# Hashed attention and two gated layers on one core: q and k arrive as columns, twice over, and the hash bits come from one fp32 product a head

## The chip, the cores and the metric

One core of one Trainium2 chip runs the whole program. The metric is device time in microseconds (us). The kernel before takes 852.57 us, the median of 3 runs (852.17 to 852.62). TensorE is PE in the rows (its weight loads are PEld), VectorE is DVE, ScalarE is ACT, GpSimd is POOL, and SyncE, which issues all transfers, is SP. SBUF is the on-chip memory, PSUM the accumulators that TensorE writes.

## The reference

q, k and v are 2 batches x 8 heads x 768 rows x 64. Six hash bits put each row of q and of k in one of 64 buckets; a score counts only where the buckets agree. Two layers with a gate follow.

```
q_bucket = sum over i of 2^i * ((q @ proj)[..., i] > 0)      # k_bucket likewise
scores   = where(q_bucket == k_bucket, q @ k.T / 8, -1e9)
attn     = exp(scores - max);  attn /= sum(attn) + 1e-9
x        = (attn @ v), heads side by side: 1536 x 512
xn       = x / sqrt(mean(x*x) + 1e-6) * rms_g
y        = (silu(xn @ w_gate) * (xn @ w_val)) @ w_out        # 512 -> 1536 -> 512
h        = y @ w2_in;  out = where(h > 0, h, exp(h) - 1) @ w2_out   # 512 -> 2048 -> 512
```

## The kernel before

**Numbers.** Products run in fp32r, a shorter float that TensorE takes at a quarter of fp32's passes. To keep precision each operand is split into a "hi" (the cast) and a "lo" (the value less its cast), and the products of the parts are summed.

**Stages.** Heads are taken in 8 pairs. For each pair there is a *preparation*, which makes the score operands `tq` and `tk` of both heads, then 12 score blocks (128 rows of q against 768 of k; matmul `ps_s` L477, maximum `nm` L484 on VectorE, exponential L494 on ScalarE), the transposes of the probabilities (`ps_p` L522), their split into `pt` (L530 and L534, or L539, L543 and L546 by way of GpSimd), and the product with v (`ps_v` L569). When 4 pairs are done, a batch is normalized (`norm`, and `post` for each pair). The two layers follow (`ps_h` L908, `ps_y` L993, `ps_o` L1048) in 5 + 6 groups of weights; the weights come as float64 words, are put together as fp32 in `wf` by VectorE (L814 to L834), cast to `whi` (L855) and split to `wlo` on GpSimd (L859).

**A pair's preparation.** q and k come with rows on the partitions (`raw`, L276). `twice` (L334, GpSimd) copies each 64-wide row beside itself. `prep_T` transposes 128x128 blocks on TensorE (`ps_t`, L350), so that 128 partitions hold the 64 columns twice. From PSUM ScalarE makes hi (L356), VectorE makes lo (L361, one operand in PSUM and one in SBUF), and GpSimd copies halves about (`again` L368, `across` L371). `prep_bits` (L398, L403) multiplies the operands with `pj`, three products of parts a head and half; `prep_count` (L419, L428, L430) turns the bits into the 64 mask rows that stand in the operands' other half. A score block needs all of these of its head. Pair j + 1 is prepared while pair j is scored.

**What sets the order.** Each piece of work is a task with an engine, a time, what it reads and writes, and a priority. `Plan.order` (L77) walks through the tasks and gives each engine the one that can start first, the lowest priority number first among equals; it holds back tasks for which no buffer is free. The order comes out as a fixed list for each engine, and each engine takes its list strictly in turn. `OFF` (L33) holds the offsets to the priorities, by stage and pair. The buffers are `slot` (24 of 6 KB a partition: operands, probabilities, weights, layer inputs), `h3` (9 of 3 KB: `rd`, `vn`, `pf`, `wf` and others), and in PSUM 4 banks and 2 double banks.

Of the kernel before, what the change touches and what calls it, by code (L numbers as in the profile page):

```python
# [32 lines left out]
OFF = {'S': [-0.746, -0.843, -1.864, 66.85, -0.744, -0.758, -0.224, -0.41], 'max': [86.06, 128.957, 190.513, 53.124, 102.143, -5.035, -10.834, 24.749], 'exp': [119.567, 67.059, 76.291, 2.774, 75.069, 56.662, -35.846, 43.868], 'T': [0.573, 0.48, 0.307, 0.831, 0.703, 1.127, 1.259, 1.321], 'hi': [36.303, -33.663, 1.961, -57.136, 22.322, 57.959, -91.469, -121.974], 'lo': [-34.121, 9.653, 32.465, -109.77, -12.636, -87.223, -67.192, -11.818], 'V': [2.027, 1.953, 1.894, 2.015, 1.865, 2.222, 2.417, -11.303], 'my': [76.979, -114.216, -55.16, -8.134, -134.423, -45.978, -63.486, -29.752], 'ld': [16.116, 103.645, 134.666, -130.684, 51.199, 277.906, -45.786, 44.455], 'pv': [19.903, -68.605, 49.828, -156.296, 63.827, 116.499, -168.838, 19.653], 'prep': [-0.809, -2.78, -3.346, -0.341, -0.21, -0.194, 0.226, -82.459], 'post': [4.851, 4.774, 2.643, 1.592, 3.332, 9.244, 3.712, 28.29], 'plo': [-227.264, -10.728, 0.013, -54.307, -64.379, -36.39, 74.399, -48.961], 'wc': 0.693, 'ld1': 50.459, 'norm0': -125.474, 'rush': 27.318, 'pstep': 0.316, 'qstep': 0.146, 'norm': -8.853, 'w0': 189.461, 'w0s': 3.7229545865993564e+29}  # L33
# [146 lines left out]
def kernel(  # L180
    ctx: ExitStack,
    tc: tile.TileContext,
    q: bass.AP,
    k: bass.AP,
    v: bass.AP,
    proj: bass.AP,
    w_gate: bass.AP,
# [82 lines left out]
    def load_qk(j, prio, gate=()):  # L270
        b, h0 = divmod(2 * j, H)

        def go(i, a):
            if ("raw", j) not in st:
                st["raw", j] = slot([128, 2, 2, NC, D], F32, "raw")
            nc.sync.dma_start(  # L276
                out=st["raw", j][:, i, a], in_=(q, k)[i][b, h0 + a].rearrange("(p c) d -> p c d", c=NC)
            )

        for a in range(2):  # L280
            for i in range(2):
                dma(
                    lambda i=i, a=a: go(i, a), S * D * 4, r=[("go", j - 2), *gate],
                    w=[(("slot", "raw", j), i, a)], prio=prio + 0.05 * a,
                )

    def load_v(j, prio):
        b, h0 = divmod(2 * j, H)

# [5 lines left out]

        dma(go, 2 * S * D * 4, r=[("go", j - 1)], w=[("h3", "vn", j)], prio=prio)
# [31 lines left out]
    def twice(j, a, i, prio):  # L328
        eng = FIRST[2 * a + i] if j == 0 else "Pool"

        def go():
            st["rd", j, a, i] = half([128, NC, 2, D], F32, "rd")
            cp = {"Pool": nc.gpsimd.tensor_copy, "DVE": nc.vector.tensor_copy, "ACT": nc.scalar.copy}[eng]
            cp(out=st["rd", j, a, i], in_=st["raw", j][:, i, a].unsqueeze(2).to_broadcast([128, NC, 2, D]))  # L334

        us = {"Pool": POOL_COPY, "DVE": dve(S), "ACT": act(S) + 0.04}[eng]
        plan.add(eng, us, go, [(("slot", "raw", j), i, a)], [("h3", "rd", j, a, i)], prio)

    def prep_T(j, a, i, hf, prio):
        n = NC // 2  # L340
        cs = slice(hf * HS, (hf + 1) * HS)
        sc = QSCALE if i == 0 else 1.0
        B_ = ("bank", "t", j, a, i, hf)
        up, dn = slice(0, 64), slice(64, 128)

        def pe():
            st[B_] = bank("ps_t")
            x = st["rd", j, a, i]
            for c in range(n):
                nc.tensor.transpose(  # L350
                    out=st[B_][:, c * 128:(c + 1) * 128], identity=ident,
                    in_=x[:, hf * n + c].rearrange("p a d -> p (a d)"),
                )

        def hi():
            nc.scalar.activation(out=operand(j, a, i)[:, 0, cs], in_=st[B_][:, 0:HS], func=AF.Copy, scale=sc)  # L356

        def lo():
            t = operand(j, a, i)
            m = (up, slice(0, 128))[i]  # L360
# [12 lines left out]
        plan.add("PE", n * 0.109, pe, [("h3", "rd", j, a, i), "ident"], [B_], prio, duty=0.5)
        top = [okey(j, a, i, (h, hf)) for h in ("up", "dn")]
        plan.add("ACT", act(HS), hi, [B_], top, prio)
        if i == 0:
            plan.add("DVE", dve(HS), lo, [B_], top[:1], prio)
            plan.add("Pool", POOL_HALF, again, top[1:], [okey(j, a, i, ("dup", hf))], prio)
        else:
            plan.add("DVE", dve(HS), lo, [B_, *top], [okey(j, a, i, ("lo", hf)), okey(j, a, i, ("hot", hf))], prio)  # L380
            plan.add("Pool", POOL_HALF, across, [okey(j, a, 0, ("dn", hf))], [okey(j, a, 1, ("hot", hf))], prio)
# [82 lines left out]
    def score(u, cc, prio):  # L464
# [35 lines left out]
        need = skeys(j, a, 0, c // 3) + [okey(j, a, 0, (p, c // 3)) for p in ("dup", "hot")]  # L500
        need += [k for hf in range(2) for k in [*skeys(j, a, 1, hf), okey(j, a, 1, ("hot", hf))]]
# [532 lines left out]
    def reduce_cols(g, blk, t, tt, ds, prio):  # L1034
# [45 lines left out]
    def setup():  # L1080
        make_identity(nc, ident)
        nc.gpsimd.memset(f(pj), 0.0)

    def ones_of(t, i):
        return t.rearrange("p (n t w) -> p n t w", t=2, w=2 ** i)[:, :, 1, :]

    def setup_w():
        st["wtmp"] = half([1, NB, NBK], F32, "wtmp")
        nc.vector.memset(st["wtmp"], -1.0)
        for i in range(NB):  # L1090
            nc.vector.memset(ones_of(st["wtmp"][:, i, :], i), 1.0)

    def setup_count():
        st["ctmp"] = half([1, 2, 2, NBK], F32, "ctmp")
        c = st["ctmp"]
        nc.vector.tensor_reduce(
# [170 lines left out]
```

## Time and profile before

| | |
|---|---|
| median of the runs | 852.57 us |
| span of the profiled execution | 851.1 us |
| busy in the span: TensorE, VectorE | 832.4 us (98%), 638.5 us (75%) |
| busy in the span: ScalarE, GpSimd | 444.9 us (52%), 273.3 us (32%) |
| read from memory, written | 45.09 MB, 3.15 MB |

The profile is of one execution; its span runs from the first to the last instruction. Busy time of a matmul is modelled to its end, and matmuls overlap one another, so a busy TensorE is not one at its peak. Shares over the whole span mix stages: the attention, up to about 300 us, keeps four engines occupied, and the layers behind it mainly TensorE.

### The profile page before, as it was taken

What the parts mean: (1) busy time and instruction counts of PE and PEld (TensorE: products, weight loads), DVE (VectorE), ACT (ScalarE), POOL (GpSimd) and SP (SyncE); (2) the same over time, 40 slices, a digit from 0 to 9 for tenths busy, and PEclk for the clock granted to TensorE, in tenths of its full rate; (3) what the DMA queues carried; (4) which work ended last, traced back from release to release, by engine and by line L of the source; (5) the groups of instructions that cost most, each with busy time, mean ns of one, the idle gap of its engine ahead of it and who ended that gap; (6) DMA issues with size and microseconds to landing.
All of it is one profiled execution on the core that took longest, in us unless ns stands there. A gap on an engine that the chain in (4) does not pass through costs nothing.

```text
span 851.1 us, 12464 instructions
## 1 busy us (share of the span) xinstructions
PE 832.4 (98%) x4722; PEld 736.7 (87%) x4722; DVE 638.5 (75%) x1015; ACT 444.9 (52%) x838; POOL 273.3 (32%) x289
## 2 busy tenths in 40 slices
PE   8999999998999999999999999999999999999998
PEld 7999999887998899999889898887888888888786
DVE  6999899999999987534364565579857778676754
ACT  6988988898987664432222322235444333332321
POOL 7857476789824312111011111110201101111100
PEclk9999999999999999999999999999999999999999
DMA  5102012330002200310111312213121302001003
GB/s 168 41 17 75 2 38 75 121 122 1 20 1 75 75 13 26 112 50 1 56 48 46 100 50 100 75 33 128 62 75 37 112 25 75 25 30 46 1 12 137
DMA packets 25708, 49.05 MB, mean 58 GB/s; under 512 B 2480, under 2 KB 8880, under 8 KB 25648
## 3 DMA queue, kind: packets, MB, share of 16 engines
q1 hardware_dynamic: 25648, 48.25, 17.3%
q8 instruction: 37, 0.61, 0.3%
q14 instruction: 23, 0.19, 0.1%
HBM read 45.09 MB, written 3.15 MB: 57 GB/s over the span
## 4 chain that ended last, share of the span: by engine, by line
PE 81%; DVE 13%; ACT 4%; issue 1%; POOL 1%; ACTq 0%; DVEq 0%; POOLq 0%
PE ps_h L908 37%; PE ps_o L1048 14%; PE ps_y L993 11%; PE ps_p L522 5%; PE ps_v L569 5%; PE ps_s L477 4%; DVE nm L484 3%; DVE pt L534 3%; PE ps_t L350 2%; PE ps_b L398 2%; ACT p L494 1%; ACT pt L530 1%; DVE wf L827 1%; DVE wf L834 1%; PE ps_w L1153 1%
## 5 line engine op out<-in xcount | busy, mean ns | idle before, releaser
L859 POOL TENSOR_TENSOR wlo<-wf,whi 128x768 fp32r<-128x768 f32 (+1 forms) x54 | 86.8, 1607 | 442.9 <-ACT whi L855 430.6
L908 PE MATMUL ps_h<-xn,whi 128*128 128x512 f32 (+2 forms) x768 | 190.2, 337 | 0.8 <-DVE hf L939 0.7
L908 PEld LDWEIGHTS ps_h<-xn,whi 128*128 128x128 f32 x768 | 133.5, 189 | 13.2 <-DVE hf L939 1.1
L908 PE MATMUL ps_h<-xn,wlo 128*128 128x256 f32 (+2 forms) x384 | 128.9, 336 | 0.0
L1048 PE MATMUL ps_o<-whi,h 128*128 128x512 f32 (+1 forms) x388 | 118.7, 387 | 0.8 <-DVE oa L1060 0.8
L908 PE MATMUL ps_h<-y,whi 128*128 128x512 f32 x384 | 118.2, 389 | 0.0
L933 ACT ACTIVATE sg<-ps_h 128x512 f32<-128x512 f32 (+1 forms) x87 | 50.7, 583 | 116.6 <-PE ps_h L908 114.5
L855 ACT CAST whi<-wf 128x768 fp32r<-128x768 f32 (+1 forms) x54 | 39.6, 733 | 118.2 <-DVE wf L834 118.2
L569 PE MATMUL ps_v<-pt,vv 128*128 128x256 f32 x576 | 96.8, 295 | 4.1 <-DVE pt L534 3.2
L954 ACT CAST h<-hf 128x512 fp32r<-128x512 f32 (+1 forms) x87 | 51.6, 605 | 88.1 <-DVE hf L939 49.1
L993 PE MATMUL ps_y<-h,whi 128*128 128x512 f32 (+1 forms) x312 | 91.4, 374 | 1.5 <-DVE ya L1005 1.5
L484 DVE TENSOR_REDUCE nm<-ps_s 128x1 f32<-128x768 f32 x96 | 90.6, 945 | 1.6 <-PE ps_s L477 0.9
L958 DVE TENSOR_TENSOR h<-hf,h 128x512 fp32r<-128x512 f32 (+1 forms) x87 | 71.0, 831 | 26.9 <-ACT h L954 26.2
L494 ACT ACTIVATE p<-ps_s,nm 128x768 f32<-128x768 f32 x96 | 87.2, 909 | 5.5 <-DVE nm L484 4.4
L522 PE MATMUL ps_p<-ident,p 128*128 128x128 f32 x576 | 86.0, 275 | 3.3 <-DVE pt L534 1.5
L477 PE MATMUL ps_s<-tk,tq 128*128 128x384 f32 x384 | 87.9, 350 | 0.6 <-ACT tk L428 0.4
L1048 PEld LDWEIGHTS ps_o<-whi,h 128*128 128x128 f32 x388 | 72.2, 188 | 16.4 <-DVE oa L1060 1.9
L569 PEld LDWEIGHTS ps_v<-pt,vv 128*128 128x128 f32 x576 | 79.3, 189 | 7.2 <-DVE pt L534 5.1
L908 PEld LDWEIGHTS ps_h<-y,whi 128*128 128x128 f32 x384 | 72.1, 188 | 15.0
L939 DVE TENSOR_TENSOR hf<-ps_h,sg 128x512 f32<-128x512 f32 (+1 forms) x39 | 25.2, 647 | 78.5 <-PE ps_h L908 78.5
L534 DVE TENSOR_TENSOR pt<-ps_p,pt 128x512 fp32r<-128x512 f32 x120 | 79.9, 680 | 2.7 <-ACT pt L530 1.8
L908 PEld LDWEIGHTS ps_h<-xn,wlo 128*128 128x128 f32 x384 | 72.6, 189 | 5.5
(111 smaller groups left out, 1501.0 us busy)
## 6 DMA issues: line engine op xcount, KB each, us to landing
wraw<-in_moe_w_out_dram SPq DMA_DIRECT2D x12, 768.0 KB, 4.9
wraw<-in_moe_w_in_dram SPq DMA_DIRECT2D x8, 768.0 KB, 4.6
wraw<-in_moe_w_out_dram SPq DMA_DIRECT2D x10, 512.0 KB, 4.1
raw<-in_q_dram SPq DMA_DIRECT2D x16, 192.0 KB, 3.4
raw<-in_k_dram SPq DMA_DIRECT2D x16, 192.0 KB, 3.7
vn<-in_v_dram SPq DMA_DIRECT2D x8, 384.0 KB, 3.3
wraw<-in_moe_w_gate_dram SPq DMA_DIRECT2D x4, 768.0 KB, 4.4
wraw<-in_moe_w_val_dram SPq DMA_DIRECT2D x4, 768.0 KB, 4.6
```

Source lines behind the costliest of these rows:

```text
L477: nc.tensor.matmul(st[B_][:, hf, 0:HS], lhsT=tq[:, x, c * 128:(c + 1) * 128], rhs=tk[:, x, hf * HS:(hf + 1) * HS], start=(x == 0), stop=(x ...
L484: nc.vector.tensor_reduce(out=st["nm", u, cc], in_=st[B_][:, :, 0:HS], axis=AX.XY, op=ALU.max, negate=True,)
L494: nc.scalar.activation(out=halves(st["p", u][:, cc]), in_=st.pop(B_)[:, :, 0:HS], func=AF.Exp, bias=st["nm", u, cc], scale=1.0, accum_out= ...
L522: nc.tensor.transpose(out=st[B_][:, o:o + 128], in_=p[:, cc, (2 * n + kt) * 128:(2 * n + kt + 1) * 128], identity=ident,)
L534: nc.vector.tensor_tensor(out=pt[:, 1], in0=st.pop(B_), in1=f(pt[:, 0]), op=ALU.subtract)
L569: nc.tensor.matmul(st[B_][:, 0:256], lhsT=st["vv", j][:, a, 2 * n + kt, :], rhs=pt[:, x, kt * 256:(kt + 1) * 256], start=(n == seq[0] and ...
L859: nc.gpsimd.tensor_tensor(out=l, in0=s["w"], in1=f(h), op=ALU.subtract)
L908: nc.tensor.matmul(ps[:, o:o + ln], lhsT=w[wp][:, kk, ft * 128:(ft + 1) * 128], rhs=t[xp][:, s:s + ln], start=(kk == 0 and n == 0), stop=( ...
L954: nc.scalar.copy(out=st["h", g, blk, ft][:, 0, 0:bw], in_=s["hf"])
L958: nc.vector.tensor_tensor(out=h[:, 1, 0:bw], in0=s["hf"], in1=f(h[:, 0, 0:bw]), op=ALU.subtract)
L993: nc.tensor.matmul(s["ps"][:, 0:bw], lhsT=wo[wp][:, ft, m * 128:(m + 1) * 128], rhs=h[:, xp, 0:bw], start=(ft == 0 and i == 0), stop=(ft = ...
L1048: nc.tensor.matmul(s["ps"], lhsT=h[:, xp, t * 128:(t + 1) * 128], rhs=wo[wp][:, ft, ds], start=(ft == 0 and i == 0), stop=(ft == n - 1 and ...
```

## The change

q and k are laid out before the launch: for each head three 128x768 blocks, `qk` (q's columns over k's), `kk` (k's twice) and `qq` (q's twice), 384 KB each. The hash products read `qk` as it lies in fp32, one product a head and half, with a `pj` of zeros and copies of proj that is also laid out before the launch; so is the table of signs that `prep_count` multiplies with. The score operands are cast from `kk` and `qq` in SBUF: k's hi on ScalarE and lo on VectorE, q's hi, its copy and lo all on GpSimd, 768 columns at once (384 for the first pair). The factor 1/8 moves from q to k. v and the output rows go in plain order. `twice`, `prep_T` and the building of `pj` and of the table are gone. `slot` has 22 buffers and `h3` 14. The three loads of each head wait for the first score of the pair before. `OFF` has new numbers (a line of 340 numbers, not shown).

```diff
-SLOTS, H3S, PTS = 24, 9, 4
+SLOTS, H3S, PTS = 22, 14, 4
+QENG = [("Pool", "Pool", "Pool")] * 16
+    def load_x(j, prio):
+        def go(a, x):
+            st["x", j, a, x] = half([128, S], F32, RAW[x])
+            nc.sync.dma_start(out=st["x", j, a, x], in_=heads[2 * j + a, x])
+
+        for n, (x, a) in enumerate(((0, 0), (0, 1), (1, 0), (2, 0), (1, 1), (2, 1))):
+            dma(
+                lambda x=x, a=a: go(a, x), S * 128 * 4, r=[("go", j - 1)],
+                w=[("h3", "x", j, a, x)], prio=prio + 0.05 * n,
+            )
...
+    def operand_k(j, a, cols, prio):
...
+            nc.scalar.activation(
+                out=operand(j, a, 1)[:, 0, cs], in_=st["x", j, a, 1][:, cs], func=AF.Copy, scale=QSCALE
+            )
...
+            nc.vector.scalar_tensor_tensor(
+                out=t[dn, 1, cs], in0=st["x", j, a, 1][dn, cs], scalar=QSCALE, in1=f(t[dn, 0, cs]),
+                op0=ALU.mult, op1=ALU.subtract,
             )
...
+    def operand_q(j, a, cols, prio, engs):
...
+            cast(engs[0], operand(j, a, 0)[:, 0, cs], st["x", j, a, 2][:, cs])
...
+            cast(engs[1], operand(j, a, 0)[dn, 1, cs], st["x", j, a, 2][dn, cs])
...
+            e.tensor_tensor(out=t, in0=st["x", j, a, 2][up, cs], in1=f(t), op=ALU.subtract)
...
     def prep_bits(j, hf, prio):
...
-                tq, tk = (operand(j, a, i) for i in range(2))
-                todo += [(pj[:, a, 0], tq[:, 0, cs]), (pj[:, a, 1], tk[:, 0, cs]), (pj[:, a, 2], tk[:, 1, cs])]
-            for n, (w, x) in enumerate(todo):
                 nc.tensor.matmul(
-                    st[B_][:, 0:HS], lhsT=w, rhs=x, start=(n == 0), stop=(n == len(todo) - 1)
+                    st[B_][:, 0:HS], lhsT=pj[:, a], rhs=st["x", j, a, 0][:, cs], start=(a == 0), stop=(a == 1)
                 )
...
     def prep(j, prio, step):
         p = prio
-        for a in range(2):
-            for i in range(2):
-                twice(j, a, i, p)
-                for hf in range(2):
-                    prep_T(j, a, i, hf, p)
-                    p += step
...
+        for a in range(2):
+            for cols in ((0,), (1,)) if j == 0 else ((0, 1),):
+                operand_k(j, a, cols, prio + off("opk", j) + a * off("opa", j))
+                operand_q(j, a, cols, prio + off("opq", j) + a * off("opa", j), QENG[2 * j + a])
...
-                if j + 2 < NPAIR:
-                    load_qk(j + 2, base + off("ld", j))
                 if j + 1 < NPAIR:
+                    load_x(j + 1, base + off("ld", j))
```

How the lists change shows at two places. The first is TensorE from the first pair's counts (`ps_c`) on, where the second pair is prepared beside the first scores. Before:

```order
L419 MATMUL ps_c<-bitt_83,wsel 128x384 x4
L477 MATMUL ps_s<-tk,tq 128x384 x4
L350 MATMUL ps_t<-ident,rd 128x128 x6
L477 MATMUL ps_s<-tk,tq 128x384 x4
L350 MATMUL ps_t<-ident,rd 128x128 x12
L477 MATMUL ps_s<-tk,tq 128x384 x4
L350 MATMUL ps_t<-ident,rd 128x128 x6
L522 MATMUL ps_p<-ident,p 128x128 x4
```

Now:

```order
L399 MATMUL ps_c<-bitt_82,wsel 128x384 x4
L455 MATMUL ps_s<-tk,tq 128x384 x16
L500 MATMUL ps_p<-ident,p 128x128 x12
L455 MATMUL ps_s<-tk,tq 128x384 x4
L380 MATMUL ps_b<-qk,pj 128x384 x2
L547 MATMUL ps_v<-pt,vv 128x256 x4
```

The transposes `ps_t` that stood between the scores are gone; four score blocks follow one another, and then three groups of `ps_p`.

The second place is VectorE while the sixth pair is prepared (`tq` and `tk` are its operands, the other rows work for the pair being scored). Before, its second head:

```order
L361 SCALAR_TENSOR_TENSOR tq<-ps_t,tq 64x384
L534 TENSOR_TENSOR pt<-ps_p,pt 128x512
L587 TENSOR_TENSOR ot<-ps_v,ot 64x256
L361 SCALAR_TENSOR_TENSOR tq<-ps_t,tq 64x384
L484 TENSOR_REDUCE nm<-ps_s 128x1
L534 TENSOR_TENSOR pt<-ps_p,pt 128x512
L361 SCALAR_TENSOR_TENSOR tk<-ps_t,tk 128x384
L636 TENSOR_TENSOR xT<-ot,ps_x 128x384 x2
L484 TENSOR_REDUCE nm<-ps_s 128x1
L587 TENSOR_TENSOR ot<-ps_v,ot 64x256
L534 TENSOR_TENSOR pt<-ps_p,pt 128x512
L361 SCALAR_TENSOR_TENSOR tk<-ps_t,tk 128x384
```

Now, its first head:

```order
L332 SCALAR_TENSOR_TENSOR tk<-kk,tk 64x768
L512 TENSOR_TENSOR pt<-ps_p,pt 128x512
L614 TENSOR_TENSOR xT<-ot,ps_x 128x384
L565 TENSOR_TENSOR ot<-ps_v,ot 64x256
L462 TENSOR_REDUCE nm<-ps_s 128x1
L614 TENSOR_TENSOR xT<-ot,ps_x 128x384 x2
L565 TENSOR_TENSOR ot<-ps_v,ot 64x256
L462 TENSOR_REDUCE nm<-ps_s 128x1
L512 TENSOR_TENSOR pt<-ps_p,pt 128x512 x3
L462 TENSOR_REDUCE nm<-ps_s 128x1
L385 TENSOR_SCALAR bitt_83<-ps_b 24x384
```

Four instructions a head, each with a PSUM operand, have become one of twice the columns, with both operands in SBUF.

## Rows read from the trace of the kernel before

**Rows 1.** The page, busy time of the engines over the span
```profile
PE 832.4 (98%) x4722; PEld 736.7 (87%) x4722; DVE 638.5 (75%) x1015; ACT 444.9 (52%) x838; POOL 273.3 (32%) x289
```

**Rows 2.** Busy time by stretch, under a line that names the columns
```profile
core 0: us, PE busy (x) PEld busy (x) DVE busy (x) ACT busy (x) POOL busy (x), PEclk, DMA share, GB/s
16.40:140.00 123.60, 123.14 (x913) 117.63 (x914) 116.48 (x191) 108.73 (x234) 84.67 (x110) 1.00 0.15 47
140.00:300.00 160.00, 150.37 (x1051) 138.39 (x1051) 155.53 (x246) 134.14 (x272) 104.14 (x110) 1.00 0.17 55
300.00:540.00 240.00, 240.00 (x1294) 215.12 (x1293) 137.39 (x221) 82.24 (x141) 35.55 (x24) 1.00 0.18 57
```

**Rows 3.** TensorE's waits from 16.4 to 300: us in total, times, longest
```profile
PEld ps_v L569 <- DVE pt L534: 5.1, 9, 1.5
```

**Rows 4.** Chain of waits from 180 to 220: start, us, what
```profile
187.23 0.46 DVE tq L361
...
200.97 0.37 ACT ot L583
...
206.50 0.49 ACT pf L539
...
207.04 2.35 PE ps_b L398 x12
...
217.69 0.33 PE ps_t L350 x3
```

**Rows 5.** Chain of waits of the whole span, the same columns
```profile
299.84 1.41 PE ps_z L674 x4
```

**Rows 6.** Transposes of q and k from 16.4 to 140: count, busy us, mean ns
```profile
L350 PE MATMUL ps_t<-ident,rd 128*128 128x128 f32 x96 | 15.2, 275 | 0.3 <-DVE tk L361 0.2
```

**Rows 7.** The same from 140 to 300
```profile
L350 PE MATMUL ps_t<-ident,rd 128*128 128x128 f32 x72 | 11.8, 278 | 0.6 <-DVE tq L361 0.5
```

**Rows 8.** VectorE by line from 16.4 to 300, the same columns
```profile
L834 DVE SCALAR_TENSOR_TENSOR wf<-wraw,wf 128x768 int32<-128x768 int32 x7 | 8.8, 1262 | 0.0
...
L654 DVE TENSOR_TENSOR sq<-xT 128x768 f32<-128x768 f32 x1 | 0.9, 948 | 0.0
```

**Rows 9.** Instructions in order of time from 296.5: start, us, engine, line
```profile
296.92 1.84 POOL L859 TENSOR_TENSOR wlo<-wf,whi 128x768 fp32r<-128x768 f32 x1 [6.60 <-ACT whi L855]
...
297.22 2.35 DVE L658 TENSOR_TENSOR sq<-sq 128x768 f32<-128x768 f32 x1
```

**Rows 10.** ScalarE and GpSimd by line over the span: count, busy us, mean ns
```profile
L859 POOL TENSOR_TENSOR wlo<-wf,whi 128x768 fp32r<-128x768 f32 x28 | 52.3, 1867 | 212.6 <-ACT whi L855 212.6
...
L334 POOL COPY rd<-raw 128x768 f32<-128x768 f32 x30 | 24.2, 823 | 2.8 <-DMA raw<-in_q_dram 2.1 <-PE ps_t L350 0.2
L855 ACT CAST whi<-wf 128x768 fp32r<-128x768 f32 x28 | 23.4, 837 | 44.3 <-DVE wf L834 44.2
...
L368 POOL CAST tq<-tq 64x384 fp32r<-64x384 f32 x32 | 15.7, 506 | 3.7 <-ACT tq L356 2.5
L356 ACT ACTIVATE tk<-ps_t 128x384 fp32r<-128x384 f32 x32 | 15.5, 501 | 1.9 <-PE ps_t L350 1.7
```

**Rows 11.** Start of the program, in order of time
```profile
0.73 0.39 SPq L276 DMA_DIRECT2D raw<-in_q_dram  x1
...
5.80 0.83 ACT L334 COPY rd<-raw 128x768 f32<-128x768 f32 x1 [0.32 <-DMA raw<-in_k_dram]
...
13.95 0.51 PE L419 MATMUL ps_c<-bitt,wsel 128*128 128x384 f32 x2
...
16.39 0.44 PE L477 MATMUL ps_s<-tk,tq 128*128 128x384 f32 x1 [0.44 <-ACT tk L428]
```

**Rows 12.** The stretch from 9 to 18, columns as in Rows 2
```profile
9.00:18.00 9.00, 7.52 (x44) 5.91 (x43) 6.53 (x12) 4.69 (x11) 7.54 (x13) 1.00 0.93 301
```

**Rows 13.** SyncE's waits before loads of weights: us in total, times, longest
```profile
SPq L797 <- PE ps_h L908: 179.4, 14, 38.1
```

**Rows 14.** Issues of a weight load: count, KB each, median us to landing
```profile
wraw<-in_moe_w_in_dram SPq DMA_DIRECT2D x8, 768.0 KB, 4.6
```

More of the change, by code (lines that the diff above doesn't have):

```diff
@@ L182 @@
     tc: tile.TileContext,
-    q: bass.AP,
-    k: bass.AP,
+    heads: bass.AP,
     v: bass.AP,
     proj: bass.AP,
+    table: bass.AP,
     w_gate: bass.AP,
@@ L326, in okey @@
         return (("slot", ("tq", "tk")[i], j, a), part)
[L328 to L353, printed above, removed]
+    up, dn = slice(0, 64), slice(64, 128)
@@ L355, in hi @@
+    def operand_k(j, a, cols, prio):
+        cs = slice(cols[0] * HS, (cols[-1] + 1) * HS)
+        X_ = ("h3", "x", j, a, 1)
+        n = HS * len(cols)
         def hi():
[L356 removed]
+            nc.scalar.activation(
+                out=operand(j, a, 1)[:, 0, cs], in_=st["x", j, a, 1][:, cs], func=AF.Copy, scale=QSCALE
+            )
         def lo():
[L359 to L360 removed]
+            t = operand(j, a, 1)
@@ L373, in prep_T @@
[L373 to L381, printed above, removed]
@@ L406, in bits @@
             )
-        need = [k for a in range(2) for i in range(2) for k in skeys(j, a, i, hf)]
-        need += [okey(j, a, 1, ("hot", hf)) for a in range(2)]
-        plan.add("PE", 6 * mm(HS) + 0.07, pe, need + ["pj"], [B_], prio)
+        plan.add("PE", 8 * mm(HS) - 0.05, pe, [*(("h3", "x", j, a, 0) for a in range(2)), "pj"], [B_], prio)
         plan.add("DVE", dve(HS), bits, [B_, "bitt"], [(("bits", j), hf)], prio)
@@ L499, in score @@
         w = [B_] + ([("go", j)] if (a, i, cc) == (0, 0, 0) else [])
-        need = skeys(j, a, 0, c // 3) + [okey(j, a, 0, (p, c // 3)) for p in ("dup", "hot")]
-        need += [k for hf in range(2) for k in [*skeys(j, a, 1, hf), okey(j, a, 1, ("hot", hf))]]
+        need = [okey(j, a, 0, (p, c // 3)) for p in ("hi", "lo", "dup", "hot")]
+        need += [okey(j, a, 1, (p, hf)) for hf in range(2) for p in ("hi", "lo", "hot")]
         plan.add("PE", 4 * mm(HS) + 0.02, pe, need, w, prio + off("S", j))
@@ L1081, in setup @@
         make_identity(nc, ident)
[L1082 to L1096, printed above, removed]
-            out=c[:, 1, 0], in_=st["wtmp"].rearrange("o i n -> o n i"), axis=AX.X, op=ALU.add
-        )
-        nc.vector.tensor_scalar(
-            out=c[:, 0], in0=c[:, 1, 0].unsqueeze(1).to_broadcast([1, 2, NBK]), scalar1=-0.5,
-            scalar2=1.0 - 0.5 * NB, op0=ALU.mult, op1=ALU.add,
-        )
-        nc.vector.tensor_scalar(
-            out=c[:, 1], in0=c[:, 0], scalar1=-1.0, scalar2=None, op0=ALU.add
-        )
@@ L1143, with ld_table @@
-    plan.add("Pool", 0.25, setup2, [], ["wsel0"], -29.5)
-    plan.add("ACT", 2.9, setup_bits, ["ident"], ["bitt"], -29)
+    def ld_table():
+        st["wtmp"] = half([128, 2, 128], F32, "wtmp")
+        nc.sync.dma_start(out=st["wtmp"], in_=table)
+    plan.add("ACT", 0.02, lambda: nc.scalar.preload_act_table_set("natural_log_exp_and_others"), [], ["tab"], -40, tab="exp")
+    plan.add("Pool", 1.22, setup, [], ["ident"], -30)
+    plan.add("DVE", 1.9, setup_bits, [], ["bitt"], -29)
     plan.add("Pool", 0.2, setup3, [], ["ones"], -28)
-    for a in range(2):
-        dma(lambda a=a: ld_pj(a), 2000, [], [("pjf", a)], PJP)
@@ L1148 @@
-    load_qk(0, -30)
+    dma(lambda: nc.sync.dma_start(out=pj, in_=proj), 128 * 1024, [], ["pj"], -29.9)
+    load_x(0, -30)
     def warm(n):
@@ L1237, with _laid_out @@
         plan.run()
-_INS = ['q', 'k', 'v', 'proj', 'moe_w_gate', 'moe_w_val', 'moe_w_out', 'moe_rms_g', 'moe2_w_in', 'moe2_w_out']
+_INS = ['heads', 'v', 'proj', 'table', 'moe_w_gate', 'moe_w_val', 'moe_w_out', 'moe_rms_g', 'moe2_w_in', 'moe2_w_out']
 _OUTS = [((1536, 512), 'float32')]
+def _laid_out(np, q, k, v, proj, **rest):
+    B, H, S, D = q.shape
+    nb = proj.shape[1]
+    qt, kt = (x.transpose(0, 1, 3, 2).reshape(B * H, D, S) for x in (q, k))
+    heads = np.stack([np.concatenate(x, 1) for x in ((qt, kt), (kt, kt), (qt, qt))], 1)
+    v = v.reshape(B * H // 2, 2, S // 128, 128, D).transpose(0, 3, 1, 2, 4)
+    wide = np.zeros((2, D, 2, 128), proj.dtype)
+    table = np.zeros((128, 2, 128), np.float32)
+    for i in range(2):
+        for a in range(2):
+            o = (2 * i + a) * nb
+            wide[i, :, a, o:o + nb] = proj
+            for n in range(2 ** nb):
+                for b in range(nb):
+                    table[o + b, i, 64 * a + n] = 1.0 if n >> b & 1 else -1.0
+                table[32, i, 64 * a + n] = 1.0 - bin(n).count("1") - i
+    return dict(rest, heads=heads, v=v, proj=wide.reshape(2 * D, 2, 128), table=table)
 def kernel(**inputs):
@@ L1249 @@
     from concourse.bass_utils import run_bass_kernel_spmd as _run
+    inputs = _laid_out(_np, **inputs)
     nc = _bacc.Bacc("TRN2", target_bir_lowering=False, num_devices=1)
```

111 lines of the change are left out of this document (35 added, 76 removed).

## Prediction, made before the changed kernel ran

> **What bounds the kernel now.** I read the busy shares, then busy time by stretch, then waits and chain. TensorE is busy for 98% of the span [rows 1], but that hides two regimes. From 300 on it is busy without a gap, 240.00 of 240.00 in the first stretch of the layers, with VectorE at 137 [rows 2]; the change touches nothing there but buffers. In the attention the stretches differ. From 16.4 to 140 TensorE is busy for 123.1 of 123.6 us and VectorE for 116.5: TensorE bounds, VectorE is close behind. From 140 to 300 TensorE is busy for 150.4 of 160, and VectorE for 155.5, or 97%: VectorE bounds [rows 2]. The waits agree: what TensorE's loads wait for most in the attention is VectorE's half of the split, `pt`, 5.1 us in 9 waits [rows 3]. In one place, 201 to 207, the chain runs through ScalarE [rows 4]. The granted clock stands at 1.00 in all these stretches [rows 2], 2.4 GHz, before and, with TensorE no less dense, after.
>
> **The sum, part by part**, against the profiled 851.1 us; the median, 852.6, lies 1.5 above it, and I carry that.
>
> *TensorE, 16.4 to 140.* A pair loses 24 transposes. Three take 0.33 us on the chain [rows 4], so 24 take 2.64. It loses 12 fp32r hash products, 2.35 [rows 4], and gains 4 in fp32. The fp32 products of this trace are the norm's, two of 128x384, which the records count as four: 1.41, 0.705 each [rows 5]. Four take 2.82. The balance is 2.64 + 2.35 - 2.82 = 2.17 a pair. In this stretch 96 transposes stand [rows 6], four pairs: **-8.7**.
>
> This counts only if VectorE lets it. There a pair loses eight `tq` and `tk` splits at 0.46 [rows 4], 3.68, and gains two of 768 columns. That form, two SBUF operands and 768 columns, stands in the attention as the weights' assembly, 1.26 us [rows 8]; alone, such an operation takes 0.95 [rows 8], and beside a GpSimd one 2.35 [rows 9]. I take 1.26, the same instruction in the same stretch: 3.68 - 2.52 = 1.16 a pair. VectorE then has 116.5 - 4.6 = 111.9 in 123.6 - 8.7 = 114.9 us, 97%, what it reaches in the other stretch. It just fits.
>
> *VectorE, 140 to 300.* 72 transposes [rows 7], three pairs: 3 x 1.16 = **-3.5**. TensorE's own 3 x 2.17 = 6.5 is worth nothing here, since it idles 9.6 us already.
>
> *ScalarE, 201 to 207.* A pair loses eight casts at 0.50 and gains two of 768 columns, whose nearest row is the weights' cast at 0.84 [rows 10]: 2.3 a pair. Elsewhere VectorE or TensorE covers that. In these 6 us the chain is ScalarE's and one pair is being prepared; I take one head's share, **-1.2** (between 0 and -2.3).
>
> *GpSimd* loses four copies at 0.82 and eight half copies at about 0.51, 7.4 a pair [rows 10], and gains for each head two casts of 768 columns, nearest the 0.82 copy, and a subtraction, nearest 1.87: 2 x 3.5 = 7.0. Nothing; it is busy for 85 of 124 and 104 of 160 [rows 2], which leaves it room, but it stays there to collide with.
>
> *The start.* Before, the first transfer is issued at 0.73, the four (768 KB) have arrived when the last is used at 5.80, the counts start at 13.95 and the last piece of the first score at 16.39 [rows 11]. Now the counts need the table, the eighth transfer: 6 x 384 + 2 x 128 KB, 2.62 MB. At the 301 GB/s of a stretch in which the queues are full [rows 12] that is 8.7 us. By the same rate 768 KB are 2.6 us, so transfers count from 3.2, and the table is there at 11.9, 12.3 after its cast. The hash products and the operands of the first head are done by then. The counts start 1.7 earlier: **-1.7** (from -4, if the short rows of before were what held the rate down, to +2, if the first scores, now four in a row with only two double banks, wait for the exponentials where transposes stood between them).
>
> *Loads later on.* Six loads and v are 2.75 MB a pair, 9.1 us at that rate, and they wait for the first score of the pair before. A pair takes some 33 us, so they are hidden, but for the second: ScalarE's list has its `kk` casts behind the fourth exponential, some 5 us after the first score, and everything behind them on ScalarE waits. 0 to +4, taken at 0, since the `kk` come third and fifth of the seven.
>
> *Buffers.* Two fewer `slot`, where loads of weights already wait for a buffer behind `ps_h`, 179 us in 14 waits [rows 13]; TensorE does not feel it before [rows 2]. Taken at 0; the upper bound is a rival.
>
> *Setup, v and the output in plain order*: off the path or the same bytes, nothing.
>
> Sum: -8.7 - 3.5 - 1.2 - 1.7 = -15.1; 851.1 - 15.1 = 836.0, on the median **837**.
>
> **A rule against it.** Every split that VectorE makes of scores or operands before has one operand in PSUM. The new `lo` of k has both in SBUF, as the norm's sum had: it started at 297.22, 0.30 after a GpSimd subtraction that ended at 298.76, and took 2.35 us where its sister took 0.95 [rows 8, 9], that is, it ended about 0.8 after the other did. The Trainium skill ("SBUF — State Buffer", section "Who interferes with whom") says that a VectorE instruction with two SBUF inputs contends with a GpSimd instruction that reads SBUF, and that the one which comes second is blocked until the first is done. By that rule the trace agrees in this one row, and the new instruction pays whenever GpSimd is at work.
>
> **Rivals.**
> 1. *Slower: the new split is held by GpSimd each time.* At 2.35 a piece VectorE loses nothing: 2 x 2.35 - 3.68 = +1.02 a pair, 7.1 over seven pairs, 279.1 instead of 272.0 in the attention; at 97% that is 287.8 us where 283.6 stood, +4.2, less 1.7 at the start: 851.1 + 2.5 + 1.5 = 855. It decides from about 2.2 us a piece. For it: rows 9, and GpSimd busy for two thirds of the time with long operations. Against it: seven instructions of the form average 1.26 in the very stretch where GpSimd is busiest.
> 2. *Faster than forecast: the new split runs free at 0.95, and the new order keeps VectorE 98% busy through both stretches.* 272.0 - 7 x 1.78 = 259.5, / 0.98 = 264.8, -18.8, with the start -20.5: 832. For it: the list can now move work freely between the stretches, since preparation needs no TensorE and no PSUM. Against it: 97% is what an order reached so far.
> 3. *Weights late in the layers.* Ten changes of the weight group; a load takes 4.6 to land [rows 14], then at least a cast of 0.84 and a subtraction of 1.87 [rows 10]. If two fewer buffers make each change 1 us late: +10, 847. For it: rows 13. Against it: no gap of TensorE there now.
> 4. *Late loads at the second pair*, or no gain at the start: +3, 840.
> That the change does not do what it says is not a case: the lists show the transposes gone.
>
> **From cases to numbers.** The forecast 0.50 (829 to 845: the split at 0.95 to 1.7, the start from -4 to +2), rival 1 0.05, rival 2 0.25, rival 3 0.10, rival 4 0.10. The range 825 to 849 leaves out rival 1 and the far ends of 2 and 3. About 0.2%, 1.7 us, can be told from no change here. Faster by more: all but rival 1 and a sliver of rival 3, 0.93; within 0.02; slower 0.05.
>
> **What would show it.** Right: `ps_b` at about 0.7 a product and TensorE without gaps up to some 130; the new `tk` instruction near 1.26 on average; VectorE at 97% or more up to the last scores; the counts near 12.3; the layers without a gap, as long as now. Wrong: `tk` near 2.3 with GpSimd operations around each; gaps of TensorE at the group changes behind 300; ScalarE waiting for `kk`; VectorE below 95% in the attention, which would mean that the order, not an engine, sets the pace.

## The result, and the profile after

The changed kernel is slower. Its median is 858.5 us (857.3 to 859.5), against 852.5 (852.2 to 852.6) for the kernel before in the same comparison: ratio 1.0071, interval 1.0057 to 1.0085. The prediction was 837, range 825 to 849, with 0.05 for slower. Forecast and sign are both wrong.

The profiled execution has a span of 856.0 us against 851.1. First the page's busy shares, to be read beside [rows 1], and the stretches of [rows 2].

```profile
PE 821.1 (96%) x4498; PEld 717.9 (84%) x4498; DVE 641.9 (75%) x956; ACT 431.6 (50%) x790; POOL 283.4 (33%) x247
```

The columns of the windows are the stretch, busy time (and count) of TensorE, its weight loads, VectorE, ScalarE and GpSimd, the granted clock as a share, the DMA share, GB/s.

```profile
16.40:140.00 123.60, 117.89 (x799) 106.92 (x798) 113.19 (x166) 103.65 (x212) 85.45 (x89) 0.98 0.30 99
140.00:300.00 160.00, 141.46 (x941) 127.82 (x941) 155.97 (x223) 125.78 (x250) 110.77 (x93) 0.98 0.25 81
300.00:540.00 240.00, 239.02 (x1296) 214.94 (x1295) 140.94 (x218) 85.48 (x144) 39.64 (x25) 1.00 0.16 50
```

TensorE lost 11 us of busy time. VectorE executes 59 instructions fewer and is busy 3.4 us longer; GpSimd executes 42 fewer and is busy 10 us longer. In the first stretch TensorE was busy for 99.6% before and is now for 95.4%: it waits. VectorE is busy for 92% of that stretch (94% before) and for 97% of the second, as before. The layers are nearly as they were: 239.0 of 240 us busy.

Two things take more of VectorE than was foreseen. In the groups by line (count, busy us, mean ns, idle time before), the new low part of k stands at 1695 ns a piece, where the prediction took 1260. On GpSimd, whose time for 768 columns was taken as 0.82 us, the cast of q on 128 partitions takes 1084 ns.

```profile
L332 DVE SCALAR_TENSOR_TENSOR tk<-kk,tk 64x768 fp32r<-64x768 f32 x14 | 23.7, 1695 | 0.7 <-ACT tk L326 0.3
L347 POOL CAST tq<-qq 128x768 fp32r<-128x768 f32 x14 | 15.1, 1084 | 1.0 <-PE ps_s L455 1.0
```

The other thing is the weights' masks, which VectorE applies in place on SBUF. From 16.4 to 300 the first two rows are the kernel before, the last two the changed one: 10.8 us have become 15.6, a rise that the prediction has no term for.

```profile
L814 DVE TENSOR_SCALAR wf<-wf 128x768 f32<-128x768 f32 x8 | 5.9, 753 | 0.2 <-ACT wf L811 0.2
L820 DVE TENSOR_SCALAR wf<-wf 128x768 int32<-128x768 int32 x8 | 4.9, 612 | 0.0
L792 DVE TENSOR_SCALAR wf<-wf 128x768 f32<-128x768 f32 x8 | 7.7, 966 | 0.0
L798 DVE TENSOR_SCALAR wf<-wf 128x768 int32<-128x768 int32 x7 | 7.9, 1143 | 0.0
```

A mean hides how. Here are two of the fourteen low parts of k, each behind the GpSimd instructions around it, in order of time (start, duration):

```profile
78.28 1.82 POOL L363 TENSOR_TENSOR tq<-qq,tq 64x768 fp32r<-64x768 f32 x1
...
78.65 2.27 DVE L332 SCALAR_TENSOR_TENSOR tk<-kk,tk 64x768 fp32r<-64x768 f32 x1
...
183.11 1.83 POOL L363 TENSOR_TENSOR tq<-qq,tq 64x768 fp32r<-64x768 f32 x1
184.90 2.67 POOL L298 TENSOR_TENSOR vv<-vn,vv 128x384 fp32r<-128x384 f32 x2
...
183.12 3.59 DVE L332 SCALAR_TENSOR_TENSOR tk<-kk,tk 64x768 fp32r<-64x768 f32 x1
```

The first begins 0.37 after the start of a GpSimd subtraction that ends at 80.10, and itself ends at 80.92, 0.82 later. That is the picture of [rows 9] (0.8 behind GpSimd's end), which the prediction had before it. The second is held through two GpSimd instructions in a row, the subtraction of q and the first of v's two (0.99). Ten of the fourteen are held, and each ends 0.81 to 0.83 after the end of a GpSimd instruction. In seven of them that one works on q or stands right behind such a one; in three it is other work (`pt` twice, the norm's `sq` once). The other four take 0.95 or 0.96: nothing or only the end of a cast stands beside them, or they begin first. Then it can be GpSimd's cast that is held, 1.53 us instead of 0.82:

```profile
217.55 0.95 DVE L332 SCALAR_TENSOR_TENSOR tk<-kk,tk 64x768 fp32r<-64x768 f32 x1
...
217.66 1.53 POOL L347 CAST tq<-qq 128x768 fp32r<-128x768 f32 x1 [0.96 <-PE ps_s L455]
```

The chain of waits from 44 to 140 shows what that does. Shares of the stretch by line, the kernel before first, then after:

```profile
by line: PE ps_v L569 24.2%; PE ps_s L477 23.7%; PE ps_p L522 21.4%; PE ps_b L398 6.8%; PE ps_t L350 6.4%; DVE nm L484 3.9%; DVE pt L534 2.5%; PE ps_x L627 2.0%; ACT pt L530 1.8%; PE ps_c L419 1.3%; DVE r L605 1.2%; ACT tq L428 1.0%; ACT tk
```

```profile
by line: PE ps_s L455 14.3%; PE ps_v L547 14.3%; DVE nm L462 14.1%; PE ps_p L500 14.0%; DVE pt L512 13.7%; DVE tk L332 9.2%; issue 4.5%; DVE bitt L385 3.2%; DVE tk L410 2.3%; DVE ot L565 2.1%; DVE xT L614 1.9%; PE ps_c L399 1.6%; ACT pt L50
```

Before, the chain in this stretch is TensorE's, line after line. After, close to half of it is VectorE's, and the low part of k alone holds 9.2%. A stretch that TensorE bounded has become one in which VectorE and TensorE take turns on the chain, with neither busy all the time.

The start, in windows with the same columns:

```profile
8.00:12.00 4.00, 1.83 (x14) 1.50 (x12) 3.90 (x7) 1.01 (x3) 3.68 (x5) 1.00 0.82 294
12.00:16.00 4.00, 3.16 (x9) 2.56 (x10) 2.26 (x5) 1.81 (x4) 3.92 (x7) 0.50 1.03 414
16.00:20.00 4.00, 3.21 (x10) 2.50 (x10) 2.01 (x4) 1.98 (x4) 3.72 (x6) 0.50 0.72 283
```

TensorE idles for 2.41 us ahead of the counts at 12.23, and the granted clock falls to 0.50 (1.2 GHz), where it stood at 1.00 before [rows 12]. The same happens at the end of the attention: after 2.48 us of waiting for `hf`, products of the hidden layer run from 289.06 at a granted clock of 0.56 (288 to 292).

What TensorE waited for ahead of the counts is VectorE:

```profile
10.10 1.56 DVE L332 SCALAR_TENSOR_TENSOR tk<-kk,tk 64x384 fp32r<-64x384 f32 x2
11.69 0.49 DVE L1086 CAST wsel<-wtmp 128x256 fp32r<-128x256 f32 x1
12.23 1.65 PE L399 MATMUL ps_c<-bitt,wsel 128*128 128x384 f32 x4 [2.41 <-DVE wsel L1086]
```

The table, issued at 4.0, had landed 6.4 later, at 10.4. Its cast to `wsel` stood in VectorE's list behind two low parts of k, 0.78 us each, where the shortest of that size takes 0.56.

### The profile page after: what moved, and what is told of

Its sections match the earlier page's. It is cut to its first block, busy times and chain, and to the rows that moved or that the text cites. A ratio compares the mean times of both kernels' runs of the same rounds, so it can differ in the third digit from the quotient of the medians.

```text
span 856.0 us, 11827 instructions
## 1 busy us (share of the span) xinstructions
PE 821.1 (96%) x4498; PEld 717.9 (84%) x4498; DVE 641.9 (75%) x956; ACT 431.6 (50%) x790; POOL 283.4 (33%) x247
## 4 chain that ended last, share of the span: by engine, by line
PE 72%; DVE 18%; ACT 4%; issue 2%; POOL 2%; DMA 1%; SPq 0%; ACTq 0%; DVEq 0%; POOLq 0%
PE ps_h L886 37%; PE ps_o L1026 14%; PE ps_y L971 11%; DVE nm L462 4%; DVE pt L512 4%; PE ps_v L547 3%; PE ps_s L455 3%; PE ps_p L500 3%; DVE tk L332 3%; ACT p L472 1%; ACT pt L508 1%; DVE wf L805 1%; DVE ot L565 1%; DVE bitt L385 1%; DVE wf L812 1%
## 5 line engine op out<-in xcount | busy, mean ns | idle before, releaser
L837 POOL TENSOR_TENSOR wlo<-wf,whi 128x768 fp32r<-128x768 f32 (+1 forms) x54 | 89.9, 1673 | 438.8 <-ACT whi L833 426.1
L547 PE MATMUL ps_v<-pt,vv 128*128 128x256 f32 x576 | 92.4, 294 | 5.4 <-DVE pt L512 3.9
L455 PE MATMUL ps_s<-tk,tq 128*128 128x384 f32 x384 | 90.7, 360 | 3.7 <-ACT p L472 3.1
L472 ACT ACTIVATE p<-ps_s,nm 128x768 f32<-128x768 f32 x96 | 87.1, 907 | 12.3 <-DVE nm L462 11.0
L500 PE MATMUL ps_p<-ident,p 128*128 128x128 f32 x576 | 81.9, 276 | 8.6 <-DVE pt L512 3.2
L500 PEld LDWEIGHTS ps_p<-ident,p 128*128 128x128 f32 x576 | 66.2, 142 | 15.7 <-issue 3.4
```

The source lines that it names most:

```text
L455: nc.tensor.matmul(st[B_][:, hf, 0:HS], lhsT=tq[:, x, c * 128:(c + 1) * 128], rhs=tk[:, x, hf * HS:(hf + 1) * HS], start=(x == 0), stop=(x ...
L472: nc.scalar.activation(out=halves(st["p", u][:, cc]), in_=st.pop(B_)[:, :, 0:HS], func=AF.Exp, bias=st["nm", u, cc], scale=1.0, accum_out= ...
L500: nc.tensor.transpose(out=st[B_][:, o:o + 128], in_=p[:, cc, (2 * n + kt) * 128:(2 * n + kt + 1) * 128], identity=ident,)
L547: nc.tensor.matmul(st[B_][:, 0:256], lhsT=st["vv", j][:, a, 2 * n + kt, :], rhs=pt[:, x, kt * 256:(kt + 1) * 256], start=(n == seq[0] and ...
L837: nc.gpsimd.tensor_tensor(out=l, in0=s["w"], in1=f(h), op=ALU.subtract)
```

## The experiments

Three theories. **A**: the new low part of k and GpSimd's work on SBUF block one another, and VectorE's time is what is lost. **B**: the half clock at the start. **C**: the new priorities put something late, whatever a single instruction takes. All runs were compared with the kernel before on the same chip; differences between two experiments are of their medians.

**1. No low part of k.**
```diff
-            nc.vector.scalar_tensor_tensor(
-                out=t[dn, 1, cs], in0=st["x", j, a, 1][dn, cs], scalar=QSCALE, in1=f(t[dn, 0, cs]),
-                op0=ALU.mult, op1=ALU.subtract,
-            )
+            nc.vector.memset(f(t[dn, 1, cs]), 0.0)
```


> Leaves out the low part of k: VectorE writes zeros to the same 64x768 area, at the same place in its list, and reads nothing from SBUF. Nothing else moves. Theory A (the new low part of k and GpSimd's work block one another): the 14 instructions fall from 1.70 to about 0.70, 13.9 us of VectorE, and GpSimd's casts of q come back from 1.08 to about 0.82; the attention, bound by VectorE in its second half, gives back 8 to 13 us: 846 to 851. Theory B (the start at half clock is what was lost) and theory C (the new list brings the norm and the first weights late, whatever a single instruction takes): at most 3 us, 855 or more.

845.1 us, ratio 0.9913 (0.9898 to 0.9928): 13.4 us below the changed kernel, 1 us beyond A's range and far from that of B and C. By line:

```profile
L332 DVE MEMSET tk<- 64x768 f32 x14 | 9.8, 698 | 3.0 <-issue 2.4 <-DVE pt L509 0.4 <-DVE tk L407 0.2
L344 POOL CAST tq<-qq 128x768 fp32r<-128x768 f32 x14 | 11.4, 824 | 1.0 <-PE ps_s L452 1.0
```

GpSimd's cast, which nobody touched, is back at 824 ns: the blocking went both ways. A write of zeros costs VectorE its 0.70 and an idle 0.22 ahead of it, 0.92. And the chain from 44 to 140 is mostly TensorE's again, though VectorE holds more of it than before the change (`nm` and `pt` 12.6% against 6.4%):

```profile
by line: PE ps_v L544 24.4%; PE ps_p L497 21.9%; PE ps_s L452 21.3%; DVE nm L459 6.6%; DVE pt L509 6.0%; PE ps_b L377 4.0%; DVE tk L407 2.3%; PE ps_x L602 2.0%; ACT pt L505 1.7%; DVE tq L407 1.6%; PE ps_c L396 1.2%; issue 1.2%; DVE bitt L38
```

**2. TensorE kept busy ahead of the counts.**
```diff
+            if (j, i, hf) == (0, 0, 0):
+                for _ in range(12):
+                    nc.tensor.matmul(st[B_][:, 0:128], lhsT=ident, rhs=ident, start=True, stop=True)
```


> Twelve more warm-up products stand directly ahead of the first counts on TensorE, where it idled for 2.41 us before its granted clock fell to 0.50; no other instruction moves. Theory B (the start): the rows at half clock from 12.2 to 22 (1.65 + 0.84 + 2.34 + 3.00 = 7.8 us) lose up to half, 3.9; 855 to 857. Theory A (blocking): the first scores then wait for VectorE's maxima and the exponentials, and what is won is lost again where VectorE bounds: 857.5 to 858.5, with the clock at 1.00 all the same.

858.3 us, ratio 1.0063 (1.0048 to 1.0078): no difference from the changed kernel. But the test is weaker than planned, since the low clock only moved:

```profile
12.00:16.00 4.00, 2.67 (x20) 2.34 (x18) 2.65 (x5) 1.68 (x4) 3.86 (x7) 1.00 1.03 413
16.00:20.00 4.00, 2.53 (x10) 2.03 (x10) 2.38 (x3) 2.00 (x5) 3.74 (x6) 0.71 0.75 295
20.00:24.00 4.00, 4.00 (x19) 3.90 (x17) 1.92 (x2) 2.11 (x4) 2.19 (x4) 0.50 0.02 5
```

The four scores in a row wait for operands and exponentials, TensorE idles between them (1.33 and 1.47 us), and the clock falls at 18 instead of 12. Theory A had put the time right, but with the clock at 1.00. That an order without these waits would gain nothing is not shown.

**3. The zeros written twice**, by a loop of two around the write of experiment 1.

> Leaves out the low part of k as the run before, but writes the zeros twice: about 1.40 us of VectorE a piece, close to the 1.70 that the real instruction takes, and without reading SBUF. If only VectorE's own time counts, 14 x 0.3 = 4 us come back: 854 to 855. If the blocking of GpSimd has a price of its own (theory A in full: its casts, its norm and the weights' low parts held up), it is below 853. Theory C: 858.

857.4 us, ratio 1.0052 (1.0035 to 1.0069): the whole gain is gone. The expectation put two writes at 1.40; with the 0.22 ahead of each they cost 1.84, so the range that was set beside it does not hold. Against experiment 1 that is 14 x 0.92 = 12.9 us more of VectorE, and 12.3 us more of time. So in this order VectorE's time counts, almost one for one. What GpSimd lost is not shown to be free: its casts stay at 826 ns here, and against the changed kernel this run has 14 x (1.84 - 1.70) = 2.0 us more of VectorE, yet takes 1.1 us less. One for one, GpSimd's side would be worth some 3 us; each median is uncertain by about 1.5.

**4. The other party taken away.** GpSimd's three operations on q write zeros and read nothing (two casts become one write each, the subtraction two):
```diff
-            cast(engs[0], operand(j, a, 0)[:, 0, cs], st["x", j, a, 2][:, cs])
+            nc.gpsimd.memset(f(operand(j, a, 0)[:, 0, cs]), 0.0)
...
```


> The other party is taken away: in the changed kernel's own order, GpSimd's three operations on q (two casts and the low part) write zeros and read nothing; q is left out of the scores. VectorE's low part of k is the real instruction. Theory A (GpSimd's reading of SBUF is what holds VectorE's instruction): its mean falls from 1.70 to 1.2 or less, 14 x 0.5 = 7 us or more of VectorE, 846 to 853. If the 1.70 belongs to the instruction itself, it stays near 1.70 and the time, with GpSimd no slower, at 856 to 859.

849.2 us, ratio 0.9965 (0.9952 to 0.9978), 9.3 below the changed kernel, in A's range. VectorE's instruction is the real one and stands in the same place in its list:

```profile
L332 DVE SCALAR_TENSOR_TENSOR tk<-kk,tk 64x768 fp32r<-64x768 f32 x14 | 15.9, 1135 | 0.7 <-ACT tk L326 0.3
```

From 1695 to 1135 ns by a change on another engine: 14 x 0.56 = 7.8 us of VectorE. The 1.70 is no property of the instruction. Singly they are clearer than the mean: eleven of the fourteen take 0.95 or 0.96, eight of them with GpSimd writing zeros beside them, and the three that stood behind `pt` and `sq` are still held (1.58, 1.50 and 2.30). One of each:

```profile
75.81 0.73 POOL L363 MEMSET tq<- 64x768 f32 x1
76.50 0.96 DVE L332 SCALAR_TENSOR_TENSOR tk<-kk,tk 64x768 fp32r<-64x768 f32 x1
76.59 0.73 POOL L364 MEMSET tq<- 64x768 f32 x1
...
142.22 1.83 POOL L637 TENSOR_TENSOR sq<-sq 128x768 f32<-128x768 f32 x1
142.57 2.30 DVE L332 SCALAR_TENSOR_TENSOR tk<-kk,tk 64x768 fp32r<-64x768 f32 x1
```

The Trainium skill ("SBUF — State Buffer", section "Who interferes with whom") says that a VectorE instruction with two SBUF inputs contends with a GpSimd one that reads SBUF, not with one that only writes it; this run agrees, with 0.96 us beside writes and 1.50 to 2.30 behind reads. GpSimd's own work on q is shorter here too (41 us against 53), so the 9.3 us are not VectorE's 7.8 alone.

**5 to 7. A list that knows of the blocking.** The order is laid twice; in the second pass the first one's start times are the priorities, and no GpSimd operation is placed beside a VectorE one on two SBUF operands:
```diff
+                    if uses[i]:
+                        t = max(t, port)
...
+            if uses[i]:
+                port = t + us
```


> All instructions of the changed kernel, in another order. The list is laid a second time with the starts of the first list as priorities and one rule more: a GpSimd operation and a VectorE operation on two SBUF operands (or in place on SBUF, as the weights' masks) are never placed side by side; the later one is put behind, and the engine takes other work meanwhile. Theory A (blocking is the price): the low part of k falls from 1.70 towards 0.95, GpSimd's casts of q from 1.08 to about 0.82 and the weights' steps beside GpSimd to about 1.0; 14 x 0.75 = 10.5 us from the first alone, so 835 to 848, faster than the kernel before. Theory C (the new priorities as such are bad, whatever blocks): the order still follows them, so 855 or more.

> The order of the run before, and zeros in place of the low part of k, which is left out (0.70 in its row and 0.22 idle ahead, some 0.92 us of VectorE). Theory A: once the list keeps the two engines apart, the real instruction costs about 0.95, so this is within 2 us of that run. If the list only shifts the blocking elsewhere, this is 5 to 12 us faster than that run, as it was with the old list (13 us).

> The kernel before, its list laid a second time by the same rule. Its splits of q and k read PSUM and are not bound by the rule; only GpSimd's work and the weights' steps and sums of VectorE are. Theory A: it gains less than the changed kernel does, 2 to 8 us: 844 to 851, and the changed kernel under the same rule is the faster of the two by some 4 to 10. If it gains as much as the changed kernel, the rule mends something that has nothing to do with the change.

858.3 us (ratio 1.0071, 1.0056 to 1.0086), 848.4 (0.9955, 0.9940 to 0.9970) and 854.0 (1.0019, 1.0010 to 1.0028). All three miss what A expected; the second fits what was set beside it for a blocking that stays (5 to 12 us faster than the first). The trace of the first shows that it does:

```profile
L350 DVE SCALAR_TENSOR_TENSOR tk<-kk,tk 64x768 fp32r<-64x768 f32 x14 | 21.0, 1507 | 0.4
L365 POOL CAST tq<-qq 128x768 fp32r<-128x768 f32 x14 | 15.0, 1084 | 2.8 <-PE ps_v L565 2.8
```

The list separates the two on paper; on the chip each engine runs through its list at its own pace, and they meet again: 1507 ns, the cast still at 1084. With zeros in the same list 9.9 us come back, against 13.4 in the old one. That is not the whole of it:

```profile
16.40:140.00 123.60, 118.39 (x799) 108.83 (x800) 112.17 (x165) 104.28 (x214) 87.76 (x91) 0.97 0.30 99
140.00:300.00 160.00, 141.92 (x938) 126.22 (x936) 147.50 (x216) 122.57 (x245) 105.15 (x92) 0.99 0.25 82
```

Up to 300 us VectorE is busy for 9.5 us less than in the changed kernel, and the time is the same. So one for one holds in the old order only, and what this order loses in its place was not followed. Theory C had 855 or more for the first, and has it; but C has no place for experiments 1 and 4, in which the order is the old one and the time falls below the kernel before. The rule alone does not cure the blocking. The kernel before gains nothing by the rule, and loses 0.19%.

**8 to 10. Priorities chosen for that rule**, without and with the low part of k on GpSimd. The second and third run do that low part as a plain subtraction on GpSimd, with the factor 1/8 moved into the exponential; the second also has q's first cast on ScalarE.

> As the run with the changed kernel and the rule, with the priorities shifted to fit a list under that rule. If the order is what is left, 2 to 6 us below that run; if VectorE's plain work bounds the attention by then, the same within 1.5.

> [...] List laid again with the rule, priorities shifted to fit. Theory A: VectorE loses 14 x 1.70 = 23.7 us of its attention work; as zeros at 0.92 gave 13 us for 10.9 less, 20 or more less should bring 835 to 845 unless GpSimd, which gains 14 x 1.84 and loses 14 x 1.08, becomes late: then a wait of the scores for GpSimd's operands shows, and 848 or more.

> As the run before, with q's casts left on GpSimd, which so gains 14 x 1.84 = 25.8 us. If VectorE alone set the pace, 835 to 846; if GpSimd is now the late one, 3 us or more above the run before.

850.8 us (0.9983, 0.9970 to 0.9995), 851.1 (0.9980, 0.9967 to 0.9994) and 850.0 (0.9985, 0.9967 to 1.0002). The first shows 1169 ns for the low part and 7.5 us less than the rule alone, 1.5 more than was expected. The other two take it off VectorE altogether (GpSimd does it in 1832 ns, and its casts are at 826) and stop at the same time, against both expectations: 851.1 lies in the range for a late GpSimd, but the wait below is for VectorE, and 850.0 lies in neither range. In the run with q's cast on ScalarE TensorE lies idle at the end of the attention, behind ten steps of the weights that stand in a row on VectorE:

```profile
258.48 0.94 PE L483 MATMUL ps_s<-tk,tq 128*128 128x384 f32 x4
268.29 1.11 PE L528 MATMUL ps_p<-ident,p 128*128 128x128 f32 x4 [8.87 <-DVE ot L593]
```

The blocking is not the new line's alone: in the changed kernel a mask of the weights, in place on SBUF, takes 2.18 us beside a GpSimd subtraction, and 0.55 where none stands beside it.

```profile
279.25 1.84 POOL L837 TENSOR_TENSOR wlo<-wf,whi 128x768 fp32r<-128x768 f32 x1
...
279.33 2.18 DVE L798 TENSOR_SCALAR wf<-wf 128x768 int32<-128x768 int32 x1
...
284.42 0.55 DVE L798 TENSOR_SCALAR wf<-wf 128x768 int32<-128x768 int32 x1
```

**11 and 12. The same two, in lists chosen to hold when durations drift.**

> The changed kernel's instructions, unchanged, in a list laid under the rule with priorities chosen so that the list also holds when durations drift by some per cent. A list can't hold two engines apart by itself, so the low part of k should come to between 1.1 and 1.4, against 1.70 and, under the rule alone, 1.51: 14 x 0.4 = 6 us, and less idle time of TensorE at the end of the attention: 843 to 851. If what is won in blocking is lost in waits again, 851 to 856.

> The low part of k on GpSimd and q's first cast on ScalarE as in the earlier run, in a list chosen to hold under drift. The earlier run left TensorE idle for 13 us from 260 to 280, where ten steps of the weights stood in a row on VectorE ahead of the next maximum. If that was all that kept it from its forecast, 838 to 846; if VectorE gives no more once it is rid of the low part, 848 to 852.

850.2 us (0.9970, 0.9959 to 0.9980), with the low part at 1184 ns, both as expected; and 848.2 us (0.9952, 0.9937 to 0.9967), the best full version of all, 4.7 us below the kernel before and 10 below the changed one. This second one has no long idle time at the end any more:

```profile
16.40:140.00 123.60, 120.72 (x817) 109.24 (x817) 104.59 (x162) 111.61 (x225) 100.10 (x94) 0.98 0.35 110
140.00:300.00 160.00, 145.69 (x962) 129.66 (x961) 139.98 (x216) 127.61 (x254) 103.05 (x89) 1.00 0.23 72
260.00:280.00 20.00, 18.97 (x143) 17.52 (x142) 17.83 (x29) 17.58 (x38) 19.28 (x22) 1.00 0.41 150
```

VectorE is down to 85% and 87% and bounds neither stretch; ScalarE at 90% and GpSimd at 81% of the first have taken over part of what it lost. The idle time at the end was not all that kept the earlier run from its forecast: 848.2 misses the 838 to 846 that was set for that case, and lies in the other range, 848 to 852, VectorE giving no more. What holds these lists near 850 was not tried. Its exponential carries the scale, which the maximum subtracted does not; the factor cancels in the division, but scores far larger than these would lose range.

## Why the prediction was wrong

**The step that failed: "That form, two SBUF operands and 768 columns, stands in the attention as the weights' assembly, 1.26 us [rows 8]" ... "I take 1.26".** It is 1.695 [line L332 above]. The mechanism was named, under "A rule against it", with the right rows [rows 9]; what was wrong was the reason for setting it aside, that seven instructions average 1.26 "in the very stretch where GpSimd is busiest". An average over a stretch says how often two instructions met that had nothing to do with each other. The new one does: kk and qq of a head are loaded one behind the other, so VectorE's low part of k and GpSimd's three operations on q can stand side by side, head by head. Ten of the fourteen are held, seven of them by that work; with it replaced by writes, only the other three are (experiment 4).

What that term is worth is measured: 14 x (1.70 - 0.92) = 10.9 us of VectorE, 13.4 of time (experiment 1); from GpSimd's side 7.8 and 9.3 (experiment 4). With either party taken away the kernel is faster than before (845.1 and 849.2).

**Rival 1 had the right place and a threshold too high.** It asked for 2.2 us a piece before the change loses, since it spread VectorE's work at a busy share of 97%. From 16.4 to 140 the changed kernel reaches 92%, with TensorE at 95%. The prediction's last paragraph had named that as a sign of being wrong: VectorE below 95% means that the order, not an engine, sets the pace. In this order a shorter instruction on VectorE still gave the time back.

**The rest of the miss.** With zeros at 0.92, below the 0.95 of a free instruction, the prediction's own arithmetic gives 851.1 - 8.7 - 3 x 1.84 - 1.2 - 1.7, that is 834 for the span, and the run shows 843.3. So of the 20 us between the forecast span, 836.0, and the measured 856.0, about 10.7 belong to the low part of k and 9.3 stand without it. The 13th, the 49th and the last of the 96 maxima on VectorE's timeline start at 46.2, 138.2 and 277.4 before, and at 42.4, 134.2 and 266.4 in that run. So:
- Up to the 49th: 4.0 gained, 3.8 of them by the 13th, against 8.7 + 1.7 = 10.4. **This term failed too.** TensorE is on the chain again from 44 to 140, and 12 transposes of p and 8 products with v more than before are done between the 13th and the 49th maximum, so a part went into work ahead of the scores. In the first part the granted clock fell: it is 0.90 on average from 16.4 to 44 in that run, 1.00 before. "With TensorE no less dense" did not hold. How the 6.4 us divide is open.
- 49th to last: 7.0 gained against 5.5 + 1.2 = 6.7. Right in size; no run tells the two terms apart.
- Last to end: 3.2 lost, against nothing predicted (3.8 in the changed kernel). Before 280 the kernel before has run 24 products of the first hidden layer, the changed one 12; these come late, and some of them at the lower clock. The new list does the first batch's norm from 227 to 271 on GpSimd, where before it was done by 198. Ahead of the `hf` that TensorE waits for, two masks of the weights are held beside GpSimd (2.18 and 2.20 us, in experiment 1 too); before, one step of the weights is (2.60). That this order is the cause was argued, not tried.

**What held.** `ps_b` was foreseen at about 0.7 a product and takes 0.65 (2.58 us for the eight records of four products in experiment 1's chain); the layers have no gap above 1 us, so rival 3 falls, and past the start no instruction of the attention waited for a load of q or k (rival 4). The counts start at 12.23, foreseen 12.3, but that is luck: the table came at 10.4, not 11.9, and VectorE's held low parts made up the difference. GpSimd "nothing" did not hold: its casts were taken at 0.82 and the 128-partition one took 1.08; what that cost is between nothing and some 3 us (experiment 3).

**Still open**: what the start would be worth without the waits of its four scores, the 6.4 us of TensorE's term, and the 3 us behind the last maximum. Two later runs, 6 and 10, show a granted clock of 1.00 from 8 to 140 and take 848.4 and 850.0, in other orders; that is no test of the start, but no run shows a gain from it.

## What to carry to other kernels

Before moving a split from a PSUM source to two SBUF sources, look at what the other engine that reads SBUF does at the same time, above all with data of the same head: price the new instruction also as held, not at a mean of unrelated ones. A rule in the list alone did not keep the two engines apart (1507 ns); priorities chosen for it did so in part (1169 and 1184). Moving the instruction to the other's engine ended the meeting. So does an operand in PSUM, as in the kernel before, where none of the 64 splits of q and k took more than 0.56. A term that rests on one engine being the bound holds only as long as the next one has room: a 97% in a sum ("it just fits") is the sign to price the failure.

## What the runs showed that was not expected

- In one and the same order, VectorE's time counts about one for one (12.3 us of time for 12.9 of VectorE); in the order of experiment 5, 9.5 us less of it up to 300 us gained nothing. GpSimd lost 14 x 0.26 = 3.6 us on its casts; whether they cost time is not settled.
- A held low part of k does nearly all its work after the other's end: ten of ten end 0.81 to 0.83 behind it, and one alone takes 0.95.
- A VectorE write of zeros of 64x768 takes 698 ns in its row, and 0.22 us of idle time stand ahead of it each time; two of them cost VectorE 1.84 us, a little more than the blocked instruction.
- Twelve small products ahead of the counts held the granted clock at 1.00 from 12 to 16, and it fell to 0.50 a few us later, after the waits of the scores.
